# A decode attention kernel: TensorE enters its loop without a wait for transfers

## The chip, the core and the metric

The kernel runs on one core of one Trainium2 chip. The core has a matrix engine (TensorE, PE in the profile), a vector engine (VectorE, DVE), a scalar engine (ScalarE, ACT), a general one (GpSimd, POOL), and a fifth that here only issues transfers (SyncE, SP). Each runs its own list of instructions in order and waits for the others by semaphores. Transfers from HBM to the on-chip memory run on 16 DMA engines that all queues share. The metric is the device time of one execution in microseconds; the time before is 672.83 us, the median of 3 runs (672.2 to 672.95).

## The reference

One step of a transformer block for four sequences: layer norm, attention over a cache of 4096 keys and values for 32 heads, and a dense layer with a mish activation.

```python
def _A_ref(x, k_cache, v_cache, wq, wo):
    B, Sq, D = x.shape                       # 4, 1, 640
    H, Dh = 32, 128
    q = (x @ wq).reshape(B, Sq, H, Dh).transpose(0, 2, 1, 3)
    scores = jnp.einsum("bhqd,bhkd->bhqk", q, k_cache) * (Dh ** -0.5)
    p = softmax(scores, axis=-1)             # over 4096 keys
    o = jnp.einsum("bhqk,bhkd->bhqd", p, v_cache)
    return o.transpose(0, 2, 1, 3).reshape(B, Sq, H * Dh) @ wo

def _B_ref(x, w1, b1, w2):
    h = jnp.einsum("bsd,df->bsf", x, w1) + b1
    sp = log1p(exp(-abs(h))) + where(h > 0, h, 0)
    return jnp.einsum("bsf,fd->bsd", h * tanh(sp), w2)

h = x + _A_ref(layernorm(x), k_cache, v_cache, wq, wo)
h2 = h + _B_ref(layernorm(h), w1, b1, w2)
```

K and V are bf16 and must each be read once: 283 MB are read in all, with the weights.

## The kernel before

**Units.** The heads are taken eight at a time, for one sequence at a time: 16 units, numbered 0 to 15. A unit's K is one transfer of 128 partitions x 32768 bf16 (8.4 MB), its V another. K2 below is the K of unit 2, and so on. Partition p holds 256 keys of one head; 16 partitions make a head.

**Three slots.** There is room for three such transfers (`slot0` to `slot2`). K of unit u goes into slot 1 for u = 0 and into slot 2u mod 3 otherwise: K0 in 1, K1 in 2, K2 in 1, K3 in 0, K4 in 2. V of unit u goes into its own K's slot once the scores are computed (V1 in slot 2, V2 in slot 1), except V0, which goes into slot 0, where the weights wq were.

**One unit.** DVE multiplies K by q in place, in 8 pieces (`times_q`, line 585). PE sums each piece over the head dimension with 8 matmuls against the identity into PSUM (`sums`, line 597), and DVE reduces what is left (line 572). Then come the row maximum (lines 634 to 674, PE's two small matmuls 643 and 665 among them) and ACT's exponentials (`exps`, line 682). V's product is late by a unit: after the sums of unit u PE does `pv` of unit u - 1 (line 707, 64 matmuls), which reads the exponentials and V of unit u - 1. The sums over partitions of unit u - 2 (`close`, lines 739 and 741) and the broadcast of the next unit's q (lines 533 to 552) stand between the pieces.

**Transfers.** All K, V and weight loads are issued by SP in this order: wq, K0, K1, V0, K2, V1, K3, V2, K4, V3, K5 and so on (`load_kv`, line 333), and behind V15 the weights of the output and of the dense layer (`load`, line 823). SP waits, ahead of each, until its slot is free: ahead of V of unit u for the last of unit u's sums (line 597), and ahead of K of unit u + 2 for `pv` of unit u - 1 (line 707).

**The order and the waits.** The kernel records every operation with what it reads and writes (`Program.add`), and `Program.plan` works out from that which operation must wait for which; `emit` writes the instructions of each engine. An operation has a `key` whose last part is the unit in whose turn it runs, a `sem` if it is a transfer (its semaphore: `slot0`, `slot1`, `slot2` ...), and `deps`, which holds, for each source, the last operation that it needs. PE's instructions of units 2 to 13 are written once, as a loop over 4 turns of three units each (`Fori`, line 200). A wait within the loop compares with a value that grows from turn to turn (line 203). Operations that lie ahead of the loop (of units 0 and 1, or with no key) have no such place in the pattern, so `plan` gathers them apart: it goes over all PE operations of the loop, all turns, and for each source keeps the latest dependence of that kind in `pe_entry`. PE waits for all of these once, ahead of the loop:

```python
        for src, d in self.pe_entry.items():
            nc.tensor.wait_ge(self.sems[src], d.count)
```

At the end of `plan` an assertion goes through the loop and holds that the entry waits and the loop's own waits together reach every dependence.

Before the change, `pe_entry` holds four sources: ACT, DVE, POOL and `slot2`, whose last operation ahead of the loop is V1. In the loop's first unit, V1 is read by `pv`, 64 sums after the entry, and there the loop has its own wait on `slot2`.

Of the kernel before, what the change touches and what calls it, by code (L numbers as in the profile page):

```python
# [21 lines left out]
class Program:  # L22
# [53 lines left out]
    def plan(self):  # L76
        by_key = {o.key: o for o in self.ops if o.key is not None}

        def shifted(o, units):
            return by_key.get((*o.key[:-1], o.key[-1] + units)) if o.key else None  # L80


        known = {e: {} for e in self.ENGINES}
        for o in self.ops:
            k = known[o.eng]
            o.waits = []
            for src, d in o.deps.items():
                if k.get(src, -1) < d.nth:
                    k[src] = d.nth
                    o.waits.append(d)  # L90


        span = self.last - self.first + 1
        assert span % self.turn == 0
        turns = span // self.turn
        self.turns = turns
        ref0 = self.first + 2 * self.turn
        body = [o for o in self.ops if self.in_loop(o) and ref0 <= o.key[-1] < ref0 + self.turn]
        self.body = body
        before, rest = [], None  # L100
        in_order = [o for o in self.ops if o.eng == "PE"]
        at = [i for i, o in enumerate(in_order) if self.in_loop(o)]
        assert at == list(range(at[0], at[0] + len(body) * turns))
        for t in range(turns):
            for p, b in enumerate(body):
                o = in_order[at[0] + t * len(body) + p]
                assert o is shifted(b, (t - 2) * self.turn), (o.key, b.key)
        self.pe_before = in_order[: at[0]]
        self.pe_after = in_order[at[0] + len(body) * turns :]
        body_waits = [[d for d in b.waits] for b in body]  # L110
        for b in body:
            for d in b.waits:
                assert d.key is not None and d.key[-1] >= self.first + self.turn, (b.key, d.key)


        loop_units = range(self.first, self.last + 1)
        for o in self.ops:
            for d in o.waits:
                d.signal = True
        for o in self.ops:  # L120
            if o.signal and o.key and o.key[-1] in loop_units:
                for u in range(self.first, self.last + 1):
                    same = by_key.get((*o.key[:-1], u))
                    if same is not None and same.sem is None:
                        same.signal = True

        self.pe_entry = {}
        first_pe = in_order[at[0]].nth
        for p in range(at[0], at[0] + len(body) * turns):
            for src, d in in_order[p].deps.items():  # L130
                if d.key is None or d.key[-1] < self.first:
                    e = self.pe_entry.get(src)
                    if e is None or e.nth < d.nth:
                        self.pe_entry[src] = d
        for d in self.pe_entry.values():
            d.signal = True

        counts = {}
        for o in self.ops:
            src = o.sem or o.eng  # L140
            if o.sem:
                counts[src] = counts.get(src, 0) + 16
            elif o.signal:
                counts[src] = counts.get(src, 0) + 1
            o.count = counts.get(src, 0)
        self.totals = counts


        self.body_waits = []
        for b, waits in zip(body, body_waits):  # L150
            out = []
            for d in waits:
                src = d.sem or d.eng
                e = shifted(d, self.turn)
                step = e.count - d.count
                assert step > 0
                for t in range(turns):
                    f = shifted(d, (t - 2) * self.turn)
                    if f is not None and f.key[-1] >= self.first:
                        assert f.count == d.count + (t - 2) * step, (b.key, d.key, t)  # L160
                base = d.count - 2 * step
                assert base > 0, (b.key, d.key)
                out.append((src, base, step))
            self.body_waits.append(out)


        level = {s: d.count for s, d in self.pe_entry.items()}
        for t in range(turns):
            for p, b in enumerate(body):
                for src, base, step in self.body_waits[p]:  # L170
                    level[src] = max(level.get(src, 0), base + t * step)
                o = in_order[at[0] + t * len(body) + p]
                for src, d in o.deps.items():
                    assert level.get(src, 0) >= d.count, (o.key, d.key, t)
# [908 lines left out]
```

## Time and profile before

| | |
|---|---|
| median of 3 runs | 672.83 us |
| the profiled execution | 673.69 us |
| its span, first to last instruction | 671.8 us |
| mean granted TensorE clock | 0.818 |
| read from HBM | 283.35 MB, 422 GB/s over the span |
| from issue to landing, median: K / V | 50.2 / 34.5 us |

How to read the lines of the profile. Times are us unless marked ns. "L597" is line 597 of the kernel. PE is the matmul, PEld its weight load, SPq the queue on which SP issues transfers. "out<-in" gives the tiles, without buffer numbers, then partitions x elements and the type; "x24" says how many equal instructions are merged. In a bracket stands how long the engine was idle before, and what ended that. The slices of the page cut the span into 40 equal parts. "PEclk" is the share of TensorE's clock that was granted. In a view by stages the columns are the stretch, its length, busy time and count of PE, PEld, DVE, ACT and POOL, then granted clock, DMA share and GB/s. A transfer is put into the stage in which its packets begin. The chain of waits follows the work that ended last back from the last instruction, from each step to what released it.

### The profile page before, as it was taken

To read this page: it belongs to the slowest core of one execution; us is meant where nothing else is said; L and a number is where in the kernel's file an instruction comes from. 1 tells how busy PE (TensorE), PEld (TensorE's weight loads), DVE (VectorE), ACT (ScalarE), POOL (GpSimd) and SP (SyncE) were. 2 spreads that over 40 slices of the span, in tenths; PEclk is the share of its full clock that TensorE was granted. 3 is DMA by queue.
4 is the path that set the end of the run, shared out by engine and by line. 5 is a ranking of instruction groups with operands and counts; after the bars stand their busy time and mean duration, and the time that the engine had idled before them with its cause. 6 is when DMAs were issued, how large, how long until landed. Compare 5 with 4: busy or idle time off the path is not lost.

```text
span 671.8 us, 6600 instructions
## 1 busy us (share of the span) xinstructions
PE 380.5 (57%) x2793; PEld 174.8 (26%) x2793; DVE 353.2 (53%) x314; ACT 88.0 (13%) x314; POOL 1.3 (0%) x10
## 2 busy tenths in 40 slices
PE   0366732887282856738184664818375481837764
PEld 0222310333031322213032321303132230313344
DVE  2078840766381836548182754728184563819501
ACT  0102020020202020110202020020202002020211
POOL 0000000000000000000000000000000000000000
PEclk9999975989596796959688796968879695978965
DMA  9999999799999999999999999999999999999997
GB/s 375 438 437 434 433 435 433 328 376 438 433 434 437 437 437 437 433 437 433 421 425 419 437 437 437 433 437 433 433 437 433 437 437 437 434 430 410 412 416 245
DMA packets 8347, 283.62 MB, mean 422 GB/s; under 512 B 835, under 2 KB 2567, under 8 KB 3208
## 3 DMA queue, kind: packets, MB, share of 16 engines
q1 hardware_dynamic: 8318, 283.35, 98.2%
q8 instruction: 12, 0.20, 0.1%
q14 instruction: 7, 0.06, 0.0%
q10 hardware_dynamic: 10, 0.01, 0.0%
HBM read 283.35 MB, written 0.01 MB: 422 GB/s over the span
## 4 chain that ended last, share of the span: by engine, by line
DMA 39%; DVE 28%; PE 20%; another core or an unknown queue 8%; SPq 3%; issue 1%
DMA slot<-in_A_k_cache_dram 33%; DVE slot L585 23%; PE bank L597 14%; PE bank L707 5%; DMA slot<-in_A_v_cache_dram 4%; DVE s_sb L572 3%; SPq L823 3%; DMA slot<-in_B_w_dram 2%; PE bank L665 0%; DVE mx L652 0%; PE bank L643 0%; DVE otn L767 0%; DVE rl L760 0%; PE bank L741 0%
## 5 line engine op out<-in xcount | busy, mean ns | idle before, releaser
L597 PE MATMUL bank<-slot,ident 128*128 128x512 bf16 x1024 | 273.9, 423 | 250.2 <-DVE slot L585 225.6
L585 DVE TENSOR_TENSOR slot<-slot,qb 128x4096 bf16<-128x4096 bf16 x128 | 288.2, 2284 | 145.4 <-DMA slot<-in_A_k_cache_dram 145.4
L597 PEld LDWEIGHTS bank<-slot,ident 128*128 128x128 bf16 x1024 | 101.5, 107 | 408.4 <-DVE slot L585 258.7
L572 DVE TENSOR_REDUCE s_sb<-bank 128x64 f32<-128x512 f32 x64 | 44.0, 688 | 74.5 <-PE bank L597 74.5
L682 ACT ACTIVATE e<-s_sb,nb 128x256 bf16<-128x256 f32 x128 | 63.1, 494 | 46.6 <-DVE nb L674 46.6
L707 PE MATMUL bank<-slot,e 128*32 128x512 bf16 x1024 | 60.7, 391 | 1.5 <-DMA slot<-in_A_v_cache_dram 1.5
L552 ACT CAST qb<-bank 128x128 bf16<-128x128 f32 x16 | 4.2, 265 | 294.5 <-PE bank L543 294.5
L727 ACT COPY o_sb<-bank 128x512 f32<-128x512 f32 x16 | 9.4, 585 | 200.2 <-PE bank L707 200.2
L707 PEld LDWEIGHTS bank<-slot,e 128*32 128x32 bf16 x1024 | 26.5, 99 | 34.1 <-issue 9.0
L652 DVE TENSOR_REDUCE mx<-bank 1x8 f32<-1x128 f32 x16 | 4.5, 279 | 39.9 <-PE bank L643 39.9
L682 ACT ACTIVATION_READ_ACCUMULATOR e<-s_sb,nb 128x1 f32 x128 | 23.9, 187 | 0.0
L741 PE MATMUL bank<-sel,o_sb 128*128 128x8 f32 x128 | 17.4, 263 | 0.0
L741 PEld LDWEIGHTS bank<-sel,o_sb 128*128 128x128 f32 x128 | 16.4, 201 | 0.0
L500 PE MATMUL bank<-xT,slot 128*128 128x4 bf16 x160 | 4.4, 168 | 11.0 <-DMA slot<-in_A_wq_dram 11.0
L665 PE MATMUL bank<-mx,nscale 1*128 1x8 f32 x32 | 6.1, 262 | 5.9 <-DVE mx L652 5.9
L760 DVE RECIPROCAL rl<-bank 128x8 f32<-128x8 f32 x16 | 3.2, 202 | 11.3 <-PE bank L741 11.3
L522 DVE COPY b1T<-bank 128x13 f32<-128x13 f32 x1 | 0.2, 172 | 14.5 <-PE bank L516 14.5
L665 PEld LDWEIGHTS bank<-mx,nscale 1*128 1x128 f32 x32 | 4.7, 183 | 10.6 <-DVE mx L652 10.6
L500 PEld LDWEIGHTS bank<-xT,slot 128*128 128x128 bf16 x160 | 4.3, 104 | 11.1 <-DMA slot<-in_A_wq_dram 11.1
L634 DVE TENSOR_REDUCE pm<-s_sb 128x1 f32<-128x256 f32 x16 | 6.7, 420 | 0.5
L739 PEld LDWEIGHTS bank<-rs,ones_f 128*128 128x128 f32 x32 | 6.1, 198 | 3.2 <-ACT o_sb L727 1.2
L643 PE MATMUL bank<-ident_f,pm 128*1 128x128 f32 x32 | 6.1, 272 | 1.2 <-DVE pm L634 1.2
(73 smaller groups left out, 69.2 us busy)
## 6 DMA issues: line engine op xcount, KB each, us to landing
slot<-in_A_v_cache_dram SPq DMA_DIRECT2D x4, 2048.0 KB, 42.5
slot<-in_A_wq_dram SPq DMA_DIRECT2D x1, 5120.0 KB, 15.5
slot<-in_A_wo_dram SPq DMA_DIRECT2D x4, 1280.0 KB, 33.8
slot<-in_B_w_dram SPq DMA_DIRECT2D x5, 432.0 KB, 29.7
slot<-in_B_w_dram SPq DMA_DIRECT2D x1, 960.0 KB, 20.4
slot<-in_B_w_dram SPq DMA_DIRECT2D x1, 640.0 KB, 19.5
slot<-in_B_w_dram SPq DMA_DIRECT2D x1, 320.0 KB, 10.9
slot<-in_A_k_cache_dram SPq DMA_DIRECT2D x16, 50.2
```

Source lines behind the costliest of these rows:

```text
L500: ins = nc.tensor.matmul(qT_ps[:, :, h], lhsT=wq_sb[:, c, h * Dh : (h + 1) * Dh], rhs=xT[:, c, :], start=(c == 0), stop=(c == DC - 1),)
L572: lambda: nc.vector.tensor_reduce(out=s_sb[:, part * RP : (part + 1) * RP], in_=s_bank[part][:, :].rearrange("p (r w) -> p r w", w=W), axi ...
L585: return nc.vector.tensor_tensor(out=kt, in0=kt, in1=qbs[u % NS][:, k * DQ : (k + 1) * DQ] .unsqueeze(1) .to_broadcast([128, RP, DQ]), op= ...
L597: ins = nc.tensor.matmul(s_bank[part][:, :].rearrange("p (r w) -> p r w", w=W), lhsT=ident[:, :], rhs=kt[:, :, d : d + W], start=(d == 0), ...
L634: lambda: nc.vector.tensor_reduce(out=pm[:, :], in_=s_sb[:, :], axis=AX.X, op=ALU.max),
L643: lambda: nc.tensor.matmul(tr_bank[0:1, 0:128], lhsT=pm[:, :], rhs=ident_f[:, :], start=True, stop=True),
L665: lambda: nc.tensor.matmul(nb_ps, lhsT=nscale[:, :], rhs=mx[:, :], start=True, stop=True),
L682: ins = nc.scalar.activation(out=e2[:, :, h, :], in_=s_sb[:, :].rearrange("p (g r) -> p g r", r=RQ), func=ACT.Exp, bias=nb[:, h : h + 1], ...
L707: ins = nc.tensor.matmul(o_bank[t : t + G * RQ, :], lhsT=e2[:, g, :, :], rhs=vt[:, g * RQ : (g + 1) * RQ, :], start=(g < CT), stop=(g >= N ...
L727: lambda: nc.scalar.copy(out=o_sb[:, :], in_=o_bank[:, :]),
L741: ins = nc.tensor.matmul(o_ps, lhsT=o_sb[:, r * Dh : (r + 1) * Dh], rhs=sel[:, r, :], start=(r == 0), stop=(r == RQ - 1),)
L823: lambda: nc.sync.dma_start(out=out_ap, in_=in_ap),
```

## The change

Where `plan` gathers the entry waits, a dependence on a transfer (`d.sem` is set) is no longer taken.

```diff
         for p in range(at[0], at[0] + len(body) * turns):
             for src, d in in_order[p].deps.items():
-                if d.key is None or d.key[-1] < self.first:
+
+                if d.sem is None and (d.key is None or d.key[-1] < self.first):
                     e = self.pe_entry.get(src)
                     if e is None or e.nth < d.nth:
                         self.pe_entry[src] = d
```

With this, `pe_entry` holds ACT, DVE and POOL, and `slot2` is gone from it. The waits within the loop and the assertion behind them are as they were. Lines after 131 move down by one.

## The prediction

> **What bounds the kernel now.** I read the page from its top: shares, slices, queues, chain.
>
> ```profile
> span 671.8 us, 6600 instructions
> PE 380.5 (57%) x2793; PEld 174.8 (26%) x2793; DVE 353.2 (53%) x314; ACT 88.0 (13%) x314; POOL 1.3 (0%) x10
> ...
> GB/s 375 438 437 434 433 435 433 328 376 438 433 434 437 437 437 437 433 437 433 421 425 419 437 437 437 433 437 433 433 437 433 437 437 437 434 430 410 412 416 245
> ...
> q1 hardware_dynamic: 8318, 283.35, 98.2%
> q8 instruction: 12, 0.20, 0.1%
> ```
>
> No engine is busy for more than 57% of the span, while the transfers keep near 435 GB/s in nearly every slice. So the kernel is bound by its stream of transfers, and time can be won only where that stream stops. Leaving out the first slice and the last, there is one such place: slices 8 and 9 (328 and 376), that is about 118 to 151 us.
>
> The list of waits (PE's and DVE's, then the issue queue's own) says what is odd there:
>
> ```profile
> DVE slot L585 <- DMA slot<-in_A_k_cache_dram: 145.4, 14, 14.4
> PE bank L597 <- DMA slot<-in_A_v_cache_dram: 24.6, 1, 24.6
> ...
> SPq L192 <- PE bank L597: 515.5, 15, 46.6
> ```
>
> Line 597 (the matmuls that sum K times q) reads no V at all, and yet PE stood once for 24.6 us ahead of it, for a V transfer. The third line says what hangs on line 597: the issue queue stands ahead of 15 of its transfers until these sums have freed a slot. The timeline has the place; its columns are start, duration, engine, line, operation and, in brackets, the idle time before and who ended it.
>
> ```profile
> 89.09 0.38 PE L665 MATMUL bank<-mx,nscale 1*128 1x8 f32 x2 [0.37 <-DVE mx L652]
> 93.56 0.19 ACT L682 ACTIVATION_READ_ACCUMULATOR e<-s_sb,nb 128x1 f32 x1
> 94.42 6.70 DVE L585 TENSOR_TENSOR slot<-slot,qb 128x4096 bf16<-128x4096 bf16 x3 [4.74 <-DMA slot<-in_A_k_cache_dram]
> 114.08 7.99 PE L597 MATMUL bank<-slot,ident 128*128 128x512 bf16 x24 [24.61 <-DMA slot<-in_A_v_cache_dram]
> 120.38 0.69 DVE L572 TENSOR_REDUCE s_sb<-bank 128x64 f32<-128x512 f32 x1 [19.27 <-PE bank L597]
> ```
>
> and the chain of waits (start, duration, what) names the transfer:
>
> ```profile
> 85.03 28.73 DMA slot<-in_A_v_cache_dram
> 113.75 0.33 issue
> ```
>
> This is unit 2, the first of PE's loop. Its K (call it K2) has landed by 94.42, and DVE multiplies. PE may start as soon as the first of those three multiplications is done, at 94.42 + 6.70/3 = 96.65, but it starts at 114.08, after V1 (the V of unit 1, issued at 85.03) has landed at 113.76: 17.4 us late. DVE then stands 19.3 us for PE.
>
> The timeline of the issue queue shows what that lateness does:
>
> ```profile
> 59.99 0.33 SPq L333 DMA_DIRECT2D slot<-in_A_k_cache_dram  x1
> 85.03 0.33 SPq L333 DMA_DIRECT2D slot<-in_A_v_cache_dram  x1
> 88.60 0.33 SPq L333 DMA_DIRECT2D slot<-in_A_k_cache_dram  x1
> 135.62 0.33 SPq L333 DMA_DIRECT2D slot<-in_A_v_cache_dram  x1
> 139.21 0.33 SPq L333 DMA_DIRECT2D slot<-in_A_k_cache_dram  x1
> 163.14 0.33 SPq L333 DMA_DIRECT2D slot<-in_A_v_cache_dram  x1
> 166.72 0.33 SPq L333 DMA_DIRECT2D slot<-in_A_k_cache_dram  x1
> 201.20 0.33 SPq L333 DMA_DIRECT2D slot<-in_A_v_cache_dram  x1
> ```
>
> In order these are K2, V1, K3, V2, K4, V3, K5, V4. V2 goes into K2's slot, so it is issued when unit 2's sums are over, at 135.62. The stages of the stream around it (PE, PEld, DVE, ACT, POOL busy, granted clock, DMA share, GB/s):
>
> ```profile
> 92.00:131.00 39.00, 14.91 (x60) 6.51 (x61) 17.28 (x12) 2.20 (x10) 0.00 (x0) 0.65 1.00 430
> 131.00:136.00 5.00, 4.10 (x28) 1.60 (x30) 3.00 (x3) 0.00 (x0) 0.00 (x0) 1.00 0.01 3
> 136.00:175.00 39.00, 25.47 (x207) 11.45 (x199) 22.48 (x21) 9.89 (x37) 0.00 (x0) 0.90 1.01 429
> 213.00:252.00 39.00, 23.01 (x143) 9.95 (x143) 21.43 (x17) 5.07 (x19) 0.00 (x0) 0.81 0.99 430
> ```
>
> Between 131 and 136 nothing moves. K3 is in, and V2 has not been issued.
>
> **The change, part by part.** The two programs differ in one place: the branch into PE's loop waits for ACT, DVE and POOL, and no longer for slot2's transfer V1. The order of work on all five engines is the same, no transfer is issued in another order, and nothing is added. The wait that V1 needs stays in the loop, ahead of unit 2's pv (line 707). Four steps follow.
>
> *The entry.* The wait itself costs nothing. What is late next there is the last entry wait, ACT's exponentials of unit 1, done at 93.56 + 0.19 = 93.75 (DVE's and POOL's are earlier). With the 0.33 us of issue that the chain shows at the entry, PE stands at line 597 by 94.1 and waits for DVE's product until 96.65. So the 17.4 us go, and ACT's end hides behind DVE; without that cover it would cost nothing until 2.6 us later.
>
> *Unit 2's sums.* How long a unit takes from its first multiplication to the issue behind its sums is seen in other units:
>
> ```profile
> 36.17 6.70 DVE L585 TENSOR_TENSOR slot<-slot,qb 128x4096 bf16<-128x4096 bf16 x3 [14.41 <-DMA slot<-in_A_k_cache_dram]
> 178.02 6.70 DVE L585 TENSOR_TENSOR slot<-slot,qb 128x4096 bf16<-128x4096 bf16 x3 [10.23 <-DMA slot<-in_A_k_cache_dram]
> 216.98 6.70 DVE L585 TENSOR_TENSOR slot<-slot,qb 128x4096 bf16<-128x4096 bf16 x3 [11.11 <-DMA slot<-in_A_k_cache_dram]
> 255.69 6.69 DVE L585 TENSOR_TENSOR slot<-slot,qb 128x4096 bf16<-128x4096 bf16 x3 [9.88 <-DMA slot<-in_A_k_cache_dram]
> 294.41 6.70 DVE L585 TENSOR_TENSOR slot<-slot,qb 128x4096 bf16<-128x4096 bf16 x3 [10.48 <-DMA slot<-in_A_k_cache_dram]
> 604.38 6.70 DVE L585 TENSOR_TENSOR slot<-slot,qb 128x4096 bf16<-128x4096 bf16 x3 [10.26 <-DMA slot<-in_A_k_cache_dram]
> ```
>
> Unit 0: 59.99 - 36.17 = 23.8. Unit 4: 201.20 - 178.02 = 23.2. So V2 is issued at 94.42 + 23.2 to 23.8 = 117.6 to 118.2, in place of 135.62. By then V1 is in (113.76), so unit 2's pv runs at once, and K4 follows 3.6 us later (139.21 - 135.62), near 121.5.
>
> *The stream.* Two transfers, one K and one V, take 255.69 - 216.98 = 38.71 and 294.41 - 255.69 = 38.72 us, so one takes 19.36. V1 in at 113.76 gives K3 in at 133.1. V2, issued 15 us before that, follows with no gap: V1, issued only 9.4 us before K2's product began, landed 113.76 - 94.42 = 19.34 us after it. V2 would be in at 152.5 and K4 at 171.9. Unit 3 then starts at 133.1 instead of 140.20, issues V3 near 156.5, and again 15 us are in hand.
>
> *The size.* From K2 to K4 (94.42 to 178.02) four transfers land in 83.60 us; without a gap they take 4 x 19.36 = 77.44. That is 6.16 lost. K5 came 38.96 after K4, 0.24 over the pair's 38.72: 6.40. From K2 to K15 (604.38) 26 transfers take 509.96 against 503.36: 6.60, though the last 0.2 of it lie at the end and have nothing to do with the entry. The lowest bound is the dead window alone: 5.0 x (1 - 3/430) = 5.0. I take 6.3, between 6.16 and 6.40, since the transfers' arrivals are what the units wait for.
>
> *Does the end follow?* All from 178.02 on waits for K's arrivals (10 to 11 us of idle in the rows above), and so does the end:
>
> ```profile
> 656.46 10.90 DMA slot<-in_B_w_dram
> 667.36 0.05 issue
> 667.40 0.71 PE bank L1024 x15
> ```
>
> The last weights land at 667.36 and the last products follow at once. Their transfers are behind the same stream on the same queue. So 6.3 us at unit 2 is 6.3 us at the end.
>
> *A rule against it.* With the change, PE is idle once more: unit 2 ends near 122 and unit 3 begins near 135, where before they joined (24 sums at full clock):
>
> ```profile
> 142.54 7.04 PE L597 MATMUL bank<-slot,ident 128*128 128x512 bf16 x24 [2.47 <-DVE slot L585]
> ```
>
> Unit 2's first 24, after an idle time, took 7.99. A cold start there costs 0.95 us, and 15 us of issue lead hide it. The Trainium skill, "TensorE: Matmul & The Clock Gate", section "HAM oscillation", says that an idle time past some 3.4 us puts the array back to half clock and that this repeats at every gap; were it on the path, the sum would be 5.3 instead of 6.3. The trace agrees on the clock (7.99 against 7.04), not on the path. The Trainium skill, "DMA: Bandwidth & Descriptors", section "Anatomy of one DMA", gives about 2.0 us of fixed cost to a transfer, for transfers issued from GpSimd; by that I estimate the gap as 135.62 - 133.1 + 2.0 = 4.5 us. The arrivals here show 6.2 and decide.
>
> *The sum.* The profiled execution has 671.8 of span and 1.9 around it, 673.69; less 6.3 it is 667.4. The median of the runs is 0.86 below the profiled one, so 672.83 - 6.3 = 666.5.
>
> **The rivals.**
>
> *Part of the gap stays.* The sums of unit 2 run at half clock all through. The first row is the stage after 114.08, the second a later group of 8:
>
> ```profile
> 114.08:119.42 5.34, 5.34 (x13) 1.94 (x14) 0.00 (x0) 0.00 (x0) 0.00 (x0) 0.50 1.08 466
> 123.33 1.90 PE L597 MATMUL bank<-slot,ident 128*128 128x512 bf16 x8 [0.24 <-DVE slot L585]
> ```
>
> That is 0.411 us a matmul against 0.238, so 64 take 26.3 us and V2 goes out near 123. That still leaves 10 us before K3 is in, more than V1 had. Against it, then; if V2 were late by half of what it is now, 669.7.
>
> *Nothing is won.* Another entry wait ends as late, or the stream catches up later. For it speaks that PE waits for three engines still; against it that all three are done by 93.75, and that the pairs after 216.98 arrive at 38.72 with no slack to catch up in. 672.8.
>
> *Slower: the loop's code isn't there.* The 24.6 us of standing also covered whatever PE must fetch to enter the loop; with 3 us of cover, a fetch queued behind transfers in flight would stand in its place. Behind one transfer it is 93.75 + 19.36 = 113.1, no gain. From 17.4 us of stall past 96.65 it decides; behind two transfers it is 132.5, 18.4 later than the 114.08 of now, all of it a longer gap: 691. Against it: all instruction traffic of queue q8 is 12 packets, 0.1% of the DMA engines, and the loop's branches show no such stall:
>
> ```profile
> L200 PEldq COMPARE_BRANCH  x4: 76/216/235, 205.4 to 553.8; - x4
> ```
>
> **How the numbers follow.** Forecast 0.87 (666.5); part of the gap stays 0.06 (669.7); nothing won 0.04 (672.8); slower 0.03 (691). The forecast's own range: savings of 6.6 to 5.0 give 666.2 to 667.8, and runs spread 0.4 us about their median (672.2 to 672.95): 665.6 to 668.3, and 0.2 more below for a unit that comes without the 0.24 of K5. That leaves out about 0.15, so it is the range. A measurement of this kernel can tell 0.2%, 1.3 us, from no change. The two first cases are faster by more: 0.93; the third is the same: 0.04; the fourth slower: 0.03.
>
> **What would show it.** PE's 24.6 us wait for V ahead of line 597 is gone and its sums begin near 96.7; V2 is issued near 118 and K4 near 122; no window near 131 to 136 is without transfers, so the 8th and 9th slice read about 433; unit 3 multiplies from about 133, K4 is in near 172, K5 near 210.6, K15 near 598; the span is 665.5. Wrong would be: an idle time at the loop's entry with another releaser or none; V2 out at 118 and yet a gap (then the issue wasn't the cause); or K4 in at 172 and the end unmoved (then something else bounds the end).

## The result, and the profile after

The changed kernel takes 668.57 us (median of 6 runs, 668.34 to 668.67), the kernel before, run beside it, 672.90 us (6 runs, 672.20 to 673.37). The ratio is 0.9936, with a 95% interval of 0.9923 to 0.9949. The change wins 4.3 us where I forecast 6.3, and the time lies 0.3 above the upper end of my range.

The page of the changed kernel (the span, then what the slices moved):

```profile
span 666.8 us, 6599 instructions
...
GB/s 378 441 436 433 440 438 429 418 429 441 429 430 436 436 440 432 425 432 440 429 429 430 440 440 436 425 432 436 429 429 432 440 440 436 422 437 405 425 414 223
...
q14 instruction: 8, 0.06, 0.0%
```

The hole in slices 8 and 9 (328 and 376 before) is gone: 418 and 429. The list of waits:

```profile
DVE slot L586 <- DMA slot<-in_A_k_cache_dram: 159.3, 15, 14.3
...
SPq L193 <- PE bank L598: 509.6, 15, 36.8
```

PE's row of 24.6 us for a V transfer is no longer in the list. The timeline has every step of the forecast (line 598 is 597 of before, 586 is 585):

```profile
96.94 6.88 PE L598 MATMUL bank<-slot,ident 128*128 128x512 bf16 x24 [7.49 <-DVE slot L586]
...
117.38 0.33 SPq L334 DMA_DIRECT2D slot<-in_A_v_cache_dram  x1
120.96 0.33 SPq L334 DMA_DIRECT2D slot<-in_A_k_cache_dram  x1
...
133.31 6.70 DVE L586 TENSOR_TENSOR slot<-slot,qb 128x4096 bf16<-128x4096 bf16 x3 [11.28 <-DMA slot<-in_A_k_cache_dram]
135.66 7.99 PE L598 MATMUL bank<-slot,ident 128*128 128x512 bf16 x24 [13.83 <-DVE slot L586]
...
172.03 6.70 DVE L586 TENSOR_TENSOR slot<-slot,qb 128x4096 bf16<-128x4096 bf16 x3 [10.16 <-DMA slot<-in_A_k_cache_dram]
210.75 6.70 DVE L586 TENSOR_TENSOR slot<-slot,qb 128x4096 bf16<-128x4096 bf16 x3 [10.75 <-DMA slot<-in_A_k_cache_dram]
...
598.09 6.69 DVE L586 TENSOR_TENSOR slot<-slot,qb 128x4096 bf16<-128x4096 bf16 x3 [9.87 <-DMA slot<-in_A_k_cache_dram]
```

Unit 2's sums begin at 96.94 and wait for DVE alone, V2 (117.38) and K4 (120.96) go out 18.2 us earlier than before, and unit 3 multiplies at 133.31 in place of 140.20. K15 is multiplied at 598.09; before it was 604.38, so 6.29 us are won there. The stages around the old hole (stretch, length, five engines, granted clock, DMA share, GB/s):

```profile
92.00:131.00 39.00, 21.61 (x143) 9.61 (x143) 21.43 (x17) 6.99 (x28) 0.00 (x0) 0.82 1.01 438
131.00:136.00 5.00, 0.34 (x1) 0.13 (x2) 2.69 (x2) 0.00 (x0) 0.00 (x0) 0.50 1.06 459
136.00:175.00 39.00, 23.01 (x145) 10.02 (x144) 21.71 (x18) 5.08 (x19) 0.00 (x0) 0.81 1.00 432
```

131 to 136 moves 459 GB/s instead of 3. And yet the chain of waits ends like this:

```profile
651.41 10.97 DMA slot<-in_B_w_dram
662.38 0.05 issue
662.42 0.72 PE bank L1025 x15
```

The last weights land at 662.38, before at 667.36: 4.98 us earlier, not 6.29. So 1.3 us went between K15's product and the last weights. The rest of the shortfall, 0.7, stands between profiled executions (673.69 and 668.67, 5.02 apart) and medians (4.33 apart). The first of these two is what the experiments are about; the second comes back at their end.

### The profile page after: what moved, and what is told of

Its sections match the earlier page's. It is cut to its first block, busy times and chain, and to the rows that moved or that the text cites. A ratio compares the mean times of both kernels' runs of the same rounds, so it can differ in the third digit from the quotient of the medians.

```text
span 666.8 us, 6599 instructions
## 1 busy us (share of the span) xinstructions
PE 378.0 (57%) x2793; PEld 173.9 (26%) x2793; DVE 353.3 (53%) x314; ACT 88.0 (13%) x314; POOL 1.3 (0%) x10
## 4 chain that ended last, share of the span: by engine, by line
DVE 31%; DMA 29%; PE 23%; another core or an unknown queue 13%; SPq 4%; issue 1%
DMA slot<-in_A_k_cache_dram 27%; DVE slot L586 26%; PE bank L598 15%; PE bank L708 6%; DVE s_sb L573 4%; SPq L824 4%; DMA slot<-in_B_w_dram 2%; PE bank L666 1%; DVE mx L653 0%; PE bank L644 0%; DVE otn L768 0%; DVE rl L761 0%; PE bank L742 0%; PE bank L1025 0%
## 5 line engine op out<-in xcount | busy, mean ns | idle before, releaser
L893 PE MATMUL bank<-slot,slot 128*128 128x4 bf16 x160 | 4.7, 166 | 3.9 <-DMA slot<-in_A_wo_dram 3.9
```

## The experiments

**What was to be told apart.** The trace has each packet of the DMA engines. Behind its share of a transfer each of the 16 engines writes one packet of four bytes, so 16 such packets show when each engine was done. At K3 of before and after they end up to 2 us apart. The table, worked out from these records, gives for each profiled execution how far the first and the last of the 16 stand behind a stream of 19.36 us a transfer (counted from the first engine's end of K0). K3 is the last transfer ahead of the old hole, V2 the first behind it, V14 the last of its size.

```
                    V2 out   K3 first/last  V2 first/last  V14 first/last  time     time - V14 last
before              135.62   -0.08 /  1.81   6.45 /  7.11   6.39 /  8.59   673.69   665.10
before_again        135.80   -0.11 /  1.85   6.38 /  7.33   6.27 /  8.78   674.00   665.22
before_look_1       134.59   -0.10 /  1.71   5.29 /  6.03   5.14 /  7.51   672.53   665.02
before_look_2       135.63   -0.07 /  1.94   6.42 /  7.14   6.28 /  8.49   673.45   664.96
after               117.38   -0.05 /  1.92  -0.05 /  1.92   0.03 /  3.07   668.67   665.60
after_again         117.24   -0.07 /  1.66  -0.08 /  1.66  -0.08 /  3.08   668.39   665.31
hold_30             129.39   -0.06 /  1.65   0.93 /  3.08   0.81 /  4.52   669.50   664.98
hold_34             131.10    0.06 /  1.88   1.80 /  3.86   1.66 /  4.09   670.36   666.27
hold_38             133.16   -0.07 /  1.82   3.93 /  4.46   3.79 /  6.20   671.26   665.06
one_engine          117.79    0.02 /  1.96   0.02 /  1.96   0.01 /  3.15   668.42   665.27
hold_38_code_1200   135.12    0.03 /  6.03   5.75 /  6.39   5.79 /  7.92   673.14   665.22
one_engine_4x       (last engine at K15: 7.45)                             672.40   664.95
code_1200           (last engine at K15: 5.84)                             671.23   665.39
more_code           (last engine at K15: 17.28)                            682.25   664.97
```

In the last three, one engine lags so far that its V14 can't be told from others' next transfer; there the last column takes the lag at K15.

*Sixteen streams* is my theory: each engine works through its own share and never catches up; a transfer has landed when its latest engine is done; and a pause lets engines that are behind draw level, so that it costs the latest engine less than the first. Taking a pause away then wins only what the latest engine stood. The table's first lines say it: over the hole the first engine of before lost 6.45 + 0.08 = 6.53, the last at most 7.11 - 1.81 = 5.30. Not all of the 6.53 was empty: V2's first packets began at 136.58, 5.85 behind the first engine's end of K3 (130.73), and each engine's first took 2.7 to 3.4 us, where a packet of 64 KB takes 2.42 in the running stream.

*One stream* is the rival: every engine loses the whole pause, and what is missing was lost at the end for another reason, or by chance.

**The two kernels once more.** First, is the shortfall reproducible? No edit.

> The kernel before, once more. Two theories stand against each other. One stream: the transfers are one stream, and what its pause costs is what the arrivals of K show (6.3 us from K2 to K15); the end came 1.3 us short of that by chance. Sixteen streams: each of the 16 DMA engines works through its own share, small transfers and instruction fetches put single engines behind, a transfer arrives with its latest engine, and a pause costs the end only what the latest engine stands idle. One stream expects spans that differ from run to run in the end part by about 1 us; sixteen streams expects the same end part again: from the start of K15's product to the end 67.4 us, span 671 to 672, time about 672.9.

> The changed kernel, once more. One stream: the end part (from the start of K15's product to the end, 68.7 us) falls back to about 67.4, and the span to 665.5. Sixteen streams: the end part is again about 68.7 us, since the engines that are behind are never let catch up; span 666.8, time 668.6.

Before 673.05 (672.53 to 674.00; against the other runs of before 0.9998, 0.9988 to 1.0008), after 668.39 (668.32 to 668.45; 0.9922, 0.9906 to 0.9939). K15's product in the profile of the one and the other:

```profile
604.70 6.69 DVE L585 TENSOR_TENSOR slot<-slot,qb 128x4096 bf16<-128x4096 bf16 x3 [10.33 <-DMA slot<-in_A_k_cache_dram]
```

```profile
598.12 6.70 DVE L586 TENSOR_TENSOR slot<-slot,qb 128x4096 bf16<-128x4096 bf16 x3 [9.87 <-DMA slot<-in_A_k_cache_dram]
```

6.58 us are won at K15 and 5.6 at the end (spans 672.1 and 666.5), so a loss of 1.0 between them comes again. Chance alone doesn't explain it.

**A pause of another length.** The changed kernel, with N exponentials into a spare tile on ACT ahead of unit 2, for which unit 2's first sums wait (34, then 30 and 38 of them; `held` is one such exponential):

```diff
-                    r=[cell, "ident"],
+                    r=[cell, "ident"] + ([("hold", 1)] if (u, part, k) == (2, 0, 0) else []),
...
+        if u == 2:
+            for i in range(34):
+                P.add(
+                    "ACT",
+                    lambda i=i: held(i % 4),
+                    r=[("s_sb", p) for p in range(NP)] + ["nb"],
+                    w=[("hold", i % 4)],
+                )
```

> The changed kernel with PE held ahead of unit 2's sums by 34 idle ACT operations (34 x 0.495 = 16.8 us from 93.75), so that V2 is issued near 131.6, between the 117.4 of the changed kernel and the 135.6 of the kernel before. One stream: a pause begins once V2 is issued after 129.3 (135.6 - 6.3), so 668.6 + 2.3 = 670.9. Sixteen streams: the latest engine is idle only once V2 is issued after 131.3 (135.6 - 4.3), so 668.6 + 0.3 = 668.9; in the profile V2 arrives late by less than the first engines stand.

> PE held by 30 idle ACT operations: 4 x 0.5 = 2 us less than with 34, so V2 is issued near 129.1, just before the first DMA engine runs dry (V2's data began 1.2 us after its issue, and the first engines end K3 near 130.5). Both theories: no pause, 668.4. A lead that must be longer than that would show here as an arrival of V2 later than 19.36 after K3.

> PE held by 38 idle ACT operations: V2 issued near 133.1, a pause of 133.1 - 129.3 = 3.8 us for the first engine. One stream: all 16 engines end V2 3.8 us behind and keep their distances (0 to 1.9 us), 668.4 + 3.8 = 672.2. Sixteen streams: the first engine 3.8 behind, the others within 0.7 of it but for one that an instruction fetch may hit (1.5 more), so the latest is only about 2.6 later than without the pause; at the end 668.4 + 3.8 + 2.3 - 3.1 = 671.4.

hold_34 took 670.35 (669.50 to 671.07; ratio 0.9951, 0.9934 to 0.9967), nearer to the one stream. The engines did draw level, 15 of them within 1.80 to 2.82, but the sixteenth stood at 3.86. One engine had a fetch of PE's code (16 KB) at 131.0, inside the pause; that it was this one fits the order of the packets and isn't shown beyond that. So the run doesn't tell the theories apart. Its time less its lag, 666.27, is 0.7 above the highest of all others, which stays open. hold_30 took 669.42 (668.50 to 669.50; 0.9938, 0.9921 to 0.9955), where both theories said 668.4: a miss for both.

```profile
129.39 0.33 SPq L336 DMA_DIRECT2D slot<-in_A_v_cache_dram  x1
```

Its V2 was out at 129.39, 1.5 us before the first engine was done with K3 (130.87), and still came 0.93 late: by this run an issue would have to lead by 1.5 + 0.9 = 2.4 us. That is an estimate: no run has a lead between this 1.5 and the 13.4 of the changed kernel. Idle time alone doesn't explain the 0.93: the engine done with K3 at 130.87 took up V2 at 130.90, but nearly all of V2's first packets took 2.5 to 4.2 us in place of 2.42. hold_38 took 670.89 (670.53 to 671.26; 0.9962, 0.9948 to 0.9976) and is nearer to the sixteen streams (671.4) than to one (672.2). Its stage in the pause:

```profile
131.00:136.00 5.00, 4.81 (x64) 2.22 (x68) 1.24 (x3) 0.00 (x0) 0.00 (x0) 1.00 0.61 213
```

Half of the stretch moves nothing, and behind it, at V2, all engines are within 3.93 to 4.46, where at K3 they were 1.9 apart. The levelling is seen; its price is still within the spread of the runs.

**One engine put behind.** If the latest engine decides, work for a single engine must cost time though 15 others have none of it. In the changed kernel each unit from 2 to 13 loads one row of 3.5 KB, which nothing uses (one packet, so one engine); then four such rows. The last two lines make a small ACT operation near the end wait for them:

```diff
         softmax(u)
+        if 2 <= u <= 13:
+            for _ in range(4):
+                P.add(
+                    "ACT",
+                    lambda u=u: nc.scalar.dma_start(
+                        out=extra[:, :], in_=k_rows[u * 1 : (u + 1) * 1, 0:1792]
+                    ),
+                    w=["extra"],
+                    sem="extra",
+                )
...
-        ["eps"],
+        ["eps", "extra"],
```

> The changed kernel with 12 more small loads (3.6 KB each, one partition, so one DMA engine each time), one in each of units 2 to 13, issued by ACT, that nothing of the stream waits for. One stream: 43 KB more at 433 GB/s is 0.1 us, 668.7. Sixteen streams: each puts the same engine behind, by 0.13 us at the least (the 3456 bytes of b1 took that) and 1.55 at the most (a 16 KB instruction fetch), 1.6 to 18 us in all on an engine that is 0 to 3 us less late than the latest; I expect about 1 us each and 674 to 680. A rise of over 1.5 us speaks for sixteen streams.

> The changed kernel with 48 small loads of 3.6 KB on one DMA engine, four in each of units 2 to 13. In the run with 12 each took 0.14 us of its engine, and put it behind by about as much at each turn, but that engine was among the first, and at V14 the latest was 3.1 us behind. One stream: 172 KB more at 433 GB/s is 0.4 us: 668.8. Sixteen streams: 48 x 0.14 = 6.9 us on one engine that was 0.2 behind, so V14 arrives 7.1 us behind the undisturbed pace, 4 us later than without: 672 to 673.

One row a unit: 668.41 (668.37 to 668.80; 0.9924, 0.9908 to 0.9941), no change against after, and a miss for my sixteen streams. A packet took only 0.14 us, the 12 of them put that engine back by some 1.7, and another was further back already (3.15): it never was the latest. Four rows a unit: 672.38 (672.11 to 672.64; 0.9987, 0.9978 to 0.9997), that is 4.0 above after_again, as the sixteen streams said (672 to 673) and not the one (668.8). The K transfers show it:

```profile
249.85 6.70 DVE L587 TENSOR_TENSOR slot<-slot,qb 128x4096 bf16<-128x4096 bf16 x3 [11.59 <-DMA slot<-in_A_k_cache_dram]
...
328.44 6.70 DVE L587 TENSOR_TENSOR slot<-slot,qb 128x4096 bf16<-128x4096 bf16 x3 [11.70 <-DMA slot<-in_A_k_cache_dram]
```

Two units take 78.59, one 39.30 instead of 38.72. The 0.58 more is four packets of 0.145 on one engine, while all 48 loads are 0.17 MB of 283.

**Instructions as load.** In after, the engine that is latest at V14 had carried fetches of 8 KB of instructions at 99.5, 359.4 and 602.4, each of which put it back by about 1.0. If such fetches are the reason, more code must cost time. The changed kernel with 3000, then 1200, stores of one element on POOL, which has nothing else to do after its first few operations:

```diff
+    for i in range(3000):
+        P.add(
+            "POOL",
+            lambda i=i: nc.gpsimd.memset(spare[:, i % 8 : i % 8 + 1], 0.0),
+            w=[("spare", i % 8)],
+        )
```

> The changed kernel with 3000 one-element memsets on POOL, which nothing waits for: more instructions to fetch in the first part of the span (192 KB if one takes 64 bytes, so some 12 fetches of 16 KB). One stream: 0.2 MB at 433 GB/s is 0.5 us: 668.9 at most. Sixteen streams: each fetch puts the engine that carries it 1.5 us behind, and no pause lets it catch up: with 12 more on 16 engines one gets two or three, so the latest at V14 is 1 to 3 us later, 669.5 to 671.5.

> The changed kernel with 1200 memsets on POOL in place of 3000. In the run with 3000 the extra fetches of 8 KB all went to one engine, about one for 128 memsets, each putting it 0.67 us behind. So 9 or 10 fetches, all within the first 60 us, put one engine 6.2 us behind by K1 or V0. One stream: 80 KB, 0.2 us: 668.6. Sixteen streams: the latest at V14 is 6.2 or somewhat more in place of 3.1, so 668.4 + 3.1 = 671.5, up to 672.

3000 stores: 681.83 (681.33 to 682.54; 1.0126, 1.0109 to 1.0143), 13.4 above after_again. The kind of effect is what the sixteen streams said, the size (669.5 to 671.5) far off: I had spread the fetches over the engines, but all of POOL's went to one. The page and the timeline:

```profile
q14 instruction: 31, 0.25, 0.1%
```

```profile
104.08 6.70 DVE L593 TENSOR_TENSOR slot<-slot,qb 128x4096 bf16<-128x4096 bf16 x3 [11.68 <-DMA slot<-in_A_k_cache_dram]
...
147.52 6.70 DVE L593 TENSOR_TENSOR slot<-slot,qb 128x4096 bf16<-128x4096 bf16 x3 [15.90 <-DMA slot<-in_A_k_cache_dram]
```

23 packets more than after's 8, 0.19 MB, and K3's product begins at 147.52 instead of 133.31; that one engine is 16.3 behind when K3 lands. The profile itself offers a rival: it puts 12% of its chain, and a wait of 14.2 us that PE ends at 106.43, down to these stores. But no operation reads what they write, they go on until 137.9, and PE starts 0.12 after DVE's first product of K2 (104.08 + 6.70/3 = 106.31). DVE's products take 6.70 us as in the other runs, so POOL's work doesn't slow them. With 1200 stores it is 671.17 (671.08 to 671.39; 0.9969, 0.9956 to 0.9981), where the sixteen streams said 671.5 and the one 668.6:

```profile
q14 instruction: 16, 0.13, 0.0%
```

**A late engine and a pause together.** If a pause lets a late engine draw level, the costs of hold_38 and code_1200 must not add. Both edits:

> The same 1200 memsets in the kernel with 38 idle ACT operations (670.9 without them), where V2 is issued near 133 and the first engine stands idle for 3.9 us after K3. If what puts an engine behind and what a pause costs simply add up, 670.9 + 3.1 = 674.0. Sixteen streams: the late engine ends K3 near 137, after V2 was issued, and doesn't stand idle at all, while the others do; at V14 the latest is about 6.2 to 7, as without the memsets, and the time 670.9 to 671.7.

673.65 (672.85 to 674.77; 1.0008, 0.9999 to 1.0018). By the time alone this is the one stream's answer (674.0). But the pause was not the one I had set: the late engine delayed K1 too, the hold began 2.5 us later, and V2 went out at 135.12 instead of 133.16, so that the first engine stood 5.75, not 3.93. The lags tell what the time can't: the late engine was 6.03 behind at K3 and no engine was more than 6.39 behind at V2. The same pause that cost the first engine 5.72 cost the late one at most 0.36. (Followed by its packets, it ended K3 at 136.89, took up V2 at once, and was 6.03 to 6.05 behind at V2: the pause cost it next to nothing.) If the two added, the latest would be at some 11.8; V14's last is at 7.92.

**Why before varies and after doesn't.** The runs of before spread from 672.2 to 674.4 over all the runs here, those of after from 668.32 to 668.67. Two more executions of before:

> The kernel before once more, for one profile. Its two profiled executions so far (673.69, 674.00) were among its slowest (672.2 to 674.4 in all), while the changed kernel's runs lie within 0.4 us. If this one is faster, the profile shows which of two it is: the pause is shorter (V2 issued earlier than 135.6; TensorE's first sums run at a clock that varies), or the pause is the same and the engines that fetches put behind are others (latest at V14 below 8.6, first engine again at 6.3 to 6.4).

> The same, once more. Both readings hold: time - latest engine's lag at V14 stays 665.0 to 665.6 as in the runs so far.

672.53 and 673.45. The first, and then the second:

```profile
114.03 7.01 PE L597 MATMUL bank<-slot,ident 128*128 128x512 bf16 x24 [24.39 <-DMA slot<-in_A_v_cache_dram]
...
134.59 0.33 SPq L333 DMA_DIRECT2D slot<-in_A_v_cache_dram  x1
```

```profile
114.24 7.84 PE L597 MATMUL bank<-slot,ident 128*128 128x512 bf16 x24 [24.79 <-DMA slot<-in_A_v_cache_dram]
...
135.63 0.33 SPq L333 DMA_DIRECT2D slot<-in_A_v_cache_dram  x1
```

With before (7.99) and before_again (8.09) these are four executions. In the one where the first 24 sums took 7.01, V2 was out a full microsecond earlier, the pause was 1.1 shorter at the first engine and the time 0.9 to 1.5 less. The time less the lag of the last engine, 664.96 to 665.22 in all four, leaves 0.26 between them. In after, sums as slow (7.99 at 135.66) stand ahead of an issue with time in hand, and the spread is gone.

The Trainium skill, "TensorE: Matmul & The Clock Gate", section "What's actually happening", says that the window of 3.4 us in which activity is counted runs freely, so that the moment at which the clock comes up varies by half a microsecond either way. The trace agrees that it varies, and here by more. Behind idle times of 24.4 to 25.3 us the granted clock went from 0.5 to 1.0 at 119.45, 119.74, 117.43 and 119.32 (before, before_again, before_look_1, before_look_2), that is 3.4 us after the first sum in before_look_1 and 5.1 to 5.6 in the others.

## Why the prediction was right, and where it failed

**The mechanism was right.** The entry: sums at 96.94 (96.65 said), and ACT's entry wait hid behind DVE's product. Unit 2's sums: V2 at 117.38 (117.6 to 118.2). The stream: unit 3 at 133.31 (133.1), K4 at 172.03 (171.9), K5 at 210.75, K15 at 598.09 (598). The cold start that I weighed came at 135.66 with 7.99 us and stayed hidden: V3 went out at 157.21, 12 us before the first engine was done with K4 (169.54). Its size I had read wrongly. The 24 sums of 7.04 at 142.54 were not at full clock; the granted clock over them was 0.76 (0.5 from 143.34 to 146.75). By the row of 8 in 1.90, 24 at full clock would take 5.7, so a cold start costs some 2.3 and not 0.95. None of the rivals came: no gap was left at V2, the end moved, and nothing stood at the loop's entry.

**The step that failed is the size's last link,** "So 6.3 us at unit 2 is 6.3 us at the end". I had read 6.3 from K arrivals against the pace of undisturbed pairs, and for K4 to K15 that held. At the end it was 5.0. Ahead of it stood "I take 6.3 ... since the transfers' arrivals are what the units wait for": this took the 16 DMA engines for one stream. At V14 the first engine came 6.39 - 0.03 = 6.36 earlier, the last one 8.59 - 3.07 = 5.52, and the end waits for the last. Why K15's product still moved by 6.29 is seen by following single engines through the packet records, by which packet joins on to which (us behind the first engine at the same transfer):

```
                                          K3     V2     V6     K15    V14
after, fetches at 99.5, 359.4, 602.4     1.13   1.14   1.05   2.06   3.03
before, fetch at 99.6                    1.30
before, fetches at 367.4, 610.3                 0.31   0.26   1.23   2.20
before, the engine furthest behind       1.89   0.65   1.88   2.07   2.20
after, the engine furthest behind        1.97   1.97   1.88   2.06   3.03
```

Each of these fetches of 8 KB puts its engine back by 0.97 to 1.0. Across the pause of before an engine can't be followed, but none is more than 0.65 behind there: whichever had the first fetch, at least half of its 1.30 is forgiven. So two of three count at V14 in before, and three in after. At K15 the furthest engine stood as far back in both, by coincidence: in before it was another one, with a fetch of its own at 598.4. So the loss shows itself only behind K15.

What is shown is the mechanism: single engines put behind set the time (one_engine_4x +4.0, code_1200 +2.8, more_code +13.4 against after_again), and a pause costs a late engine less than the others (hold_38_code_1200: 0.36 against 5.72). In 13 of the 14 profiled executions the time is the last engine's lag (at V14, in three of them at K15) plus 664.95 to 665.60, over lags from 3.1 to 17.3; hold_34 has 666.27.

**The second step that failed** is "The median of the runs is 0.86 below the profiled one, so 672.83 - 6.3 = 666.5". I took the distance as one that the changed kernel shares, but after's median is 0.10 below its profiled one. In part the distance came from the pause itself: in the profiled execution the first 24 sums took 7.99, and the gap that I measured there belonged to a long execution. In part it was the small sample: 672.83 is the median of 3 runs and 672.90 that of 6, while the later sets of 13 to 15 runs of before have medians of 673.28 to 673.37. Against one of these (673.33) the changed kernel's 668.39 wins 4.94. So of the missing 0.7 some 0.4 hangs on which runs of before were drawn.

**The sum as it should have been** goes: 6.36 at the first engine; less 0.84, which the latest engine had not lost; less 0.50 between V14 and the end (0.09 in the pair that was run again, and 664.95 to 665.60 among kernels with the same end, so no more than the scatter of the end); less 0.69 from the profiled execution to the medians of 6 runs: 4.33.

The Trainium skill, "DMA: Bandwidth & Descriptors", section "Why a DMA increments its semaphore by 16 and not by 1", has the fact that I passed by: a transfer runs on up to 16 engines that finish independently, and the semaphore counts them. The trace agrees, with ends up to 2 us apart. The 4.5 us that I had estimated from that page's fixed cost is near the 4.3 by luck: the first engine lost 6.5.

## What to carry to other kernels

Where a kernel is bound by its transfers, ask when the latest DMA engine is done, and price a pause by what that one stood: the pause also lets late engines draw level, and without it small loads and instruction fetches, which each hit one engine, add up to the end. If the stall that is removed varies from run to run, size it in an execution near the median, and expect the spread to go with it. And an issue must lead the end of the transfer ahead: 1.5 us were too little here (0.9 was lost, so some 2.4 by estimate), 13.4 were enough.

## What the hardware showed

- A fetch of 8 KB of instructions put its DMA engine back by 0.65 to 1.0 us, though its own packet took 0.31 to 0.45; PE's, of 16 KB, by some 1.5. All of POOL's fetches went to one engine, which fell 16.3 us behind in more_code. Outside a pause, no engine that was behind is seen to catch up (the 6.0 of code_1200 at K3 are still 5.8 at K15).
- A pause costs more than its empty time: each engine's first packet behind it took 2.4 to 3.5 us (before, before_look_1, hold_34, hold_38), in the running stream 2.42.
- Nothing waited for what POOL did in more_code. 0.19 MB of its code, 0.07% of what is read, made the kernel 2% slower than after_again.
